# A decode layer on one core: the first weight load in eight pieces, a wait ahead of x, and eight unused matmuls before the last waits

## The chip, the core and the metric

The kernel runs on one NeuronCore of a Trainium2 chip. Its engines are PE (matmul; PEld is its weight load), DVE, ACT and POOL (elementwise work), and SP, which here only issues DMA transfers. Sixteen DMA engines move data between HBM and the on-chip memory. The metric is the device time of one execution in microseconds (us), the median over runs; lower is better.

## What is computed

One token goes through a pre-norm layer with grouped-query attention over a cache of 65536 positions, and a gated feed-forward block:

```
x: (1, 1, 1024)   Hq, Hkv, Sk, Dh = 32, 4, 65536, 128   F = 3584   all bf16
q = layernorm(x) @ wq                        # wq 1024 x 4096
scores = q . k_cache * Dh**-0.5              # 8 query heads share one cache head
o = softmax(scores) . v_cache                # k_cache, v_cache 4 x 65536 x 128
h = x + o @ wo                               # wo 4096 x 1024
n = layernorm(h)
out = h + (gelu(n @ w_gate) * (n @ w_up)) @ w_down   # 1024 x 3584 twice, 3584 x 1024
```

The two caches are 67.1 MB each, and everything is read once: 173 MB in all.

## The kernel before

All large data go through one buffer, `ring`, of four slots of 4 MB. The slots take, in order, the two halves of `wq` (slots 0 and 1), then K tiles (slots 2 and 3, two of 4 MB a step) and V tiles (slots 0 and 1, one of 8 MB a step) for eight steps (four cache heads, two halves of the positions each), then `wo` (slots 2 and 3), `w_gate` (0 and 1), `w_up` (2 and 3) and `w_down` (0 and 1). All of these transfers stand on SP's queue in that order, and each is issued as soon as the last reader of its slot has let go.

Work is written as a list of operations. `Flow.op` (line 31) notes which operations an operation depends on by the keys it reads (`r`) and writes (`w`), `Flow.dma` (line 69) does the same for a transfer, and `Flow.issue` (line 76) walks the list once and gives each engine its instructions and semaphore waits in the order of the list. Nearly all instructions therefore carry line 95 in the profile. Only the loop over the eight attention steps on PE is written out by hand (`pe_loop`, lines 411 to 449), and so is the last product.

**The start.** Line 200 issues the load of `x` (2 KB, 32 rows) on ACT's queue; it waits for nothing. Lines 202 to 205 issue the two halves of `wq` on SP's queue, each one transfer of 128 rows (one a partition) of 32 KB, with the semaphore `r_sem[t]`; a transfer adds 16 to its semaphore when it has landed. Lines 221 and 222 issue the first two K tiles behind them. `ones_f` (a 128 x 128 block of ones for sums across partitions) is set on DVE at line 226; it is DVE's first operation. `x` is then spread over the partitions (line 289), normalised (`layernorm_cols`, line 268) into `xz`, and multiplied with the halves of `wq` (lines 315 to 319), eight groups of four matmuls of 512 columns for each half.

**The end.** `w_down` comes in four transfers (lines 580 to 586), called wa, wb0, wb1 and wb2 here: 4 MB, 2 MB, 768 KB and 256 KB, each with a semaphore of its own. After the list is issued (line 588) a second block (lines 596 to 600) makes PE wait for one of these transfers after the other and multiply its rows: `down` (line 590) does eight matmuls of 128 columns for each row a partition holds, so 128 matmuls for wa, and 64, 24 and 8 for the others. They need `actz`, the gated activations, which DVE finishes behind the `w_up` product (line 574). Lines 602 to 604 copy the result out of the accumulators and store it.

`bank[5]` is one of PE's eight accumulators; its last reader is `o_copy` (line 376) of the last attention step. `qs` (line 164) holds the spread-out queries, which nothing reads after the attention loop.

Of the kernel before, what the change touches and what calls it, by code (L numbers as in the profile page):

```python
# [16 lines left out]
class Flow:  # L17
# [13 lines left out]
    def op(self, e, call, r=(), w=(), after=(), wait=(), inc=None, dma=False, rows=None, **kw):  # L31
        i = len(self.ops)
        deps = {}

        def need(j, hard):
            o = self.ops[j]
            if o["e"] == e and not dma and not o["dma"] and (e == "pe" or not hard):
                return
            deps[j] = True

        for k in r:
            if k in self.writer:
                need(self.writer[k], True)
        for k in tuple(w) + tuple(after):
            if k in self.writer:
                need(self.writer[k], True)
            for j in self.readers.get(k, ()):
                need(j, False)
        if e == "pool":
            if self.rows[0] != rows and self.rows[1] is not None and not self.ops[self.rows[1]]["inc"]:  # L50
                deps[self.rows[1]] = True
            self.rows = rows, i
        last = {}
        for j in deps:
            o = self.ops[j]
            k = j if o["dma"] else o["e"]
            last[k] = max(last.get(k, j), j)
        deps = last.values()
        for k in r:
            self.readers.setdefault(k, []).append(i)  # L60
        for k in w:
            self.writer[k] = i
            self.readers[k] = []
        self.ops.append(dict(e=e, call=call, kw=kw, deps=sorted(deps), wait=wait, inc=inc, dma=dma))
# [44 lines left out]
def kernel(  # L109
# [13 lines left out]
    nc = tc.nc  # L123
    P = 128
# [6 lines left out]
    DC = D // P  # L131
# [14 lines left out]
    NB = 512  # L146
# [12 lines left out]
    def sb(name, shape, dtype=F32):  # L159
        return const.tile(shape, dtype, name=name)  # L160
# [3 lines left out]
    qs = sb("qs", [P, 4, NS, P + 1], BF16)  # L164
    sc = sb("sc", [P, CPH, NN, rep, NS])
    pt = sb("pt", [P, CPH, NN, rep, NS], BF16)
    bank = [psum.tile([P, NB], F32, name="bank%d" % i) for i in range(8)]
# [15 lines left out]
    def slot(i, n=1):  # L183
        return ring[:, i * CW:(i + n) * CW]

    f = Flow(nc, tc)
    op = f.op
# [4 lines left out]
    r_sem = [tc.alloc_semaphore("r_landed_%d" % i) for i in range(3)]  # L192


    wq_v = A_wq.rearrange("(p t c) n -> t p c n", t=DS, c=C4)
    assert C4 * HD == CW and DS * C4 == DC
    XU = 32
    XV = P // XU
    x_in = sb("x_in", [XU, XV, DC], BF16)
    f.dma("act", x_in[:], A_x[0, 0].rearrange("(u v j) -> u v j", u=XU, j=DC), w=["x_in"], sem=tc.alloc_semaphore("x_landed"))  # L200
    wq_tiles = []
    for t in range(DS):
        wv = slot(t).rearrange("p (c n) -> p c n", c=C4)
        f.dma("sp", wv, wq_v[t], w=["R%d" % t], sem=r_sem[t])
        wq_tiles.append(wv)
    k_v = [A_k_cache[0, g].rearrange("(p n) d -> p n d", p=P) for g in range(Hkv)]
    v_v = [A_v_cache[0, g].rearrange("(p n) d -> p n d", p=P) for g in range(Hkv)]
# [14 lines left out]
        k_load(0, p)  # L222


    ones_f = sb("ones_f", [P, P])
    op("dve", "memset", w=["ones_f"], ap=ones_f[:], constant=1.0)
    neg_half = sb("neg_half", [P, 1])
    op("dve", "memset", w=["neg_half"], ap=neg_half[:], constant=-0.5)
    ident_bf = sb("ident_bf", [P, P], BF16)
# [93 lines left out]
    for q in range(4):  # L323
        op("pe", "matmul", r=["q_bf"] + ["esel"], w=["B5"], out=qsel_ps[:, :, q, :], lhsT=esel[:, q, :], rhs=q_bf[:],
           start=True, stop=True)
# [162 lines left out]
    for dq in range(OQ):  # L488
        op("pe", "matmul", r=["o_sb", "osel"], w=["B4"], out=o2_ps, lhsT=osel[:, dq, :], rhs=o_sb[:, dq * Hq:(dq + 1) * Hq],
           start=(dq == 0), stop=(dq == OQ - 1))  # L490
# [8 lines left out]
    FA = CW // D  # L499
    FB = FC - FA  # L500
    at_ps = bank[6][:]
    wv = slot(2, 2).rearrange("p (c n) -> p c n", c=Hq)
    f.dma("sp", wv, A_wo.rearrange("(p c) n -> p c n", p=P), w=["R2", "R3"], wait=done, sem=r_sem[2])
    for c in range(Hq):
        for s in range(DS):
            q = 2 * (c % 2) + s
            op("pe", "matmul", r=["o2z", "R2", "R3"], w=["B6"], out=at_ps[32 * q:32 * q + 32, :], lhsT=o2z[:, c, :],
               rhs=wv[:, c, :].rearrange("k (p s c) -> k s p c", s=DS, c=C4)[:, s], start=(c < 2), stop=(c >= Hq - 2), tile_position=(0, 32 * q))
# [55 lines left out]
    for j in range(DC):  # L564
        op("pe", "matmul", r=["hb", "sel16"], w=["B2"], out=d_ps[:, j:OB:DC], lhsT=hb[:, j, :], rhs=sel16[:],
           start=False, stop=False, skip_group_check=True)
# [15 lines left out]
    for i, z in enumerate((FB - FZ, FZ - 1, 1)):  # L582
        part = wb[:, e0:e0 + z, :]
        s = (r_sem[1], k_sem[0], k_sem[1])[i]
# [5 lines left out]
    def down(a_row, w_row):  # L590
        for j in (0, 4, 1, 5, 2, 6, 3, 7):
            q, m = divmod(orow[j], 32)
            nc.tensor.matmul((d_ps, d_odd)[q // 2][32 * q:32 * q + 32, :], lhsT=a_row[:, AZ - m:AZ - m + 32], rhs=w_row[:, j * OB:(j + 1) * OB],  # L593
                             start=False, stop=False, skip_group_check=True, tile_position=(0, 32 * q))

    with tc.tile_critical(no_gpsimd_drain=True):
        for w_rows, a0, n, at, sem in parts:
            nc.tensor.wait_ge(sem, at)
            for e in range(n):
                down(actz[:, a0 + e, :], w_rows[:, e, :])  # L600
# [34 lines left out]
```

## Time and profile before

| | us |
|---|---|
| median of 3 runs (lowest, highest) | 410.23 (409.99, 410.27) |
| the profiled execution's own time | 410.4 |
| its span, first to last instruction | 408.3 |
| PE busy, 1639 matmuls | 233.4 |
| DVE busy | 202.6 |
| ACT busy | 39.5 |
| POOL busy | 19.2 |
| one 128 x 4096 transpose of K on DVE (32 of them) | 4.418 |
| `x`: median from issue to landing | 2.1 |
| a half of `wq`: median from issue to landing | 16.8 |
| a 4 MB K tile: median from issue to landing | 24.6 |

The span is shorter than the time of the execution by 2.1 us, which lie around the instructions. Busy times of different engines overlap. The clock column of the profile, PEclk, is the share of TensorE's full clock that was granted; its mean over the span is 0.776. A landing is the moment at which the last of the sixteen DMA engines has reported its share.

### The profile page before, as it was taken

The page shows a single profiled execution, that of the slowest core. Times are in us where ns is not written, and L with a number is a line of the kernel's source. Part 1 is how long each engine was busy: PE and PEld are TensorE (multiplying, and loading weights), DVE is VectorE, ACT ScalarE, POOL GpSimd, SP SyncE. Part 2 cuts the span into 40 slices and gives each one's busy share as a digit, 9 for nine tenths or more (in the row PEclk, how much of TensorE's full clock was granted, in tenths as well). Part 3 has the DMA queues.
Part 4 walks back from the last instruction along what each step waited for, and adds up shares of the span by engine and source line. Part 5 has one row for each costly group of instructions (what it writes and reads, how often), then busy time and mean ns, then how long its engine had stood idle before and what let it go on. Part 6 is the DMA issues. An engine that isn't in the chain of part 4 may idle for free. (4 is left out here: it accounts for less than half of the span.)

```text
span 408.3 us, 3895 instructions
## 1 busy us (share of the span) xinstructions
PE 233.4 (57%) x1639; PEld 105.8 (26%) x1639; DVE 202.6 (50%) x174; ACT 39.5 (10%) x141; POOL 19.2 (5%) x39
## 2 busy tenths in 40 slices
PE   1331864684667368736973585558557737355356
PEld 1110322231322133213321232223223213132325
DVE  4016780886089327924881697087608941021110
ACT  1000003001300300030003000400030030000000
POOL 6010000001000000010000001000000000011000
PEclk9955895699669876976797899679866997565565
DMA  8999999999999999999999999999999999899994
GB/s 337 433 424 445 424 453 411 459 411 431 440 459 417 411 441 478 417 404 421 498 417 392 430 443 433 417 459 417 427 433 469 411 417 494 386 440 440 400 422 198
DMA packets 4815, 173.12 MB, mean 424 GB/s; under 512 B 580, under 2 KB 584, under 8 KB 840
## 3 DMA queue, kind: packets, MB, share of 16 engines
q1 hardware_dynamic: 4760, 173.02, 98.4%
q8 instruction: 5, 0.08, 0.1%
q14 instruction: 2, 0.02, 0.0%
q10 hardware_dynamic: 48, 0.00, 0.0%
HBM read 173.02 MB, written 0.00 MB: 424 GB/s over the span
## 5 line engine op out<-in xcount | busy, mean ns | idle before, releaser
L95 DVE STREAM_TRANSPOSE ktb<-ring 128x4096 f32<-128x4096 f32 x32 | 141.1, 4418 | 82.8 <-DMA ring<-in_A_k_cache_dram 82.8
L427 PE MATMUL bank<-ktb,qs 128*128 128x512 bf16 x512 | 132.9, 419 | 60.3 <-PEq L413 60.3
L427 PEld LDWEIGHTS bank<-ktb,qs 128*128 128x128 bf16 x512 | 51.6, 104 | 138.4 <-issue 93.0
L439 PE MATMUL bank<-ring,pt 128*32 128x512 bf16 x512 | 46.6, 543 | 36.5 <-PEq L413 36.5
L95 ACT ACTIVATE pt<-sc,nb 128x256 bf16<-128x256 f32 x64 | 31.5, 493 | 254.8 <-DVE nb L95 254.8
L439 PEld LDWEIGHTS bank<-ring,pt 128*32 128x32 bf16 x512 | 19.4, 131 | 60.4 <-issue 57.5
L95 DVE STREAM_TRANSPOSE sc<-bank 128x512 f32<-128x512 f32 x32 | 22.3, 695 | 24.9 <-PE bank L427 24.9
L95 PE MATMUL bank<-ring,xz 128*32 128x512 bf16 (+1 forms) x192 | 18.3, 565 | 24.0 <-DMA ring<-in_A_wq_dram 13.3
L95 DVE STREAM_TRANSPOSE ktb<-bank 128x512 f32<-128x512 f32 (+1 forms) x6 | 4.0, 672 | 37.3 <-PE bank L95 37.0
L95 DVE TENSOR_REDUCE mx<-sc 128x8 f32<-128x1536 f32 (+1 forms) x16 | 19.5, 1220 | 0.5
L95 POOL COPY qs<-qsel 32x128 bf16<-32x128 bf16 x16 | 7.8, 490 | 237.4 <-PE bank L427 216.4
L95 PEld LDWEIGHTS bank<-ring,xz 128*32 128x32 bf16 x192 | 7.0, 137 | 33.8 <-DMA ring<-in_A_wq_dram 14.2
L95 ACT ACTIVATION_READ_ACCUMULATOR pt<-sc,nb 128x1 f32 x64 | 11.9, 186 | 0.0
L448 PE MATMUL bank<-sel,acc_sb 128*128 128x8 f32 x64 | 8.2, 255 | 6.2 <-PEq L413 6.2
L431 PE MATMUL bank<-ident_f,mx 128*8 128x128 f32 x8 | 2.2, 269 | 14.6 <-PEq L413 14.6
L448 PEld LDWEIGHTS bank<-sel,acc_sb 128*128 128x128 f32 x64 | 7.7, 191 | 10.0 <-issue 10.0
L95 PE MATMUL bank<-ring,ktb 128*32 128x512 bf16 x64 | 6.0, 548 | 6.8 <-DMA ring<-in_A_wo_dram 6.8
L593 PE MATMUL bank<-ring,ktb 128*32 128x128 bf16 x224 | 6.6, 311 | 5.4 <-DMA ring<-in_B_w_down_dram 5.4
L95 ACT COPY acc_sb<-bank 128x512 f32<-128x512 f32 x8 | 4.7, 586 | 49.2 <-PE bank L439 49.2
L95 DVE TENSOR_TENSOR h_col<-bank,x_col 128x8 f32<-128x8 f32 x1 | 0.2, 166 | 15.2 <-PE bank L95 15.2
L95 PE MATMUL bank<-sel,ktb 128*128 128x16 f32 (+1 forms) x24 | 5.6, 374 | 3.5 <-DVE bank L95 2.7
L593 PEld LDWEIGHTS bank<-ring,ktb 128*32 128x32 bf16 x224 | 5.8, 144 | 6.4 <-DMA ring<-in_B_w_down_dram 6.1
(83 smaller groups left out, 55.2 us busy)
## 6 DMA issues: line engine op xcount, KB each, us to landing
ring<-in_A_k_cache_dram SPq DMA_DIRECT2D x16, 4096.0 KB, 24.6
ring<-in_A_wq_dram SPq DMA_DIRECT2D x2, 4096.0 KB, 16.8
ring<-in_B_w_gate_dram SPq DMA_DIRECT2D x1, 7168.0 KB, 27.8
ring<-in_B_w_up_dram SPq DMA_DIRECT2D x1, 7168.0 KB, 27.7
ring<-in_B_w_down_dram SPq DMA_DIRECT2D x1, 4096.0 KB, 20.9
ring<-in_B_w_down_dram SPq DMA_DIRECT2D x1, 2048.0 KB, 25.4
ring<-in_B_w_down_dram SPq DMA_DIRECT2D x1, 768.0 KB, 26.1
ring<-in_B_w_down_dram SPq DMA_DIRECT2D x1, 256.0 KB, 26.2
```

Source lines behind the costliest of these rows:

```text
L95: ins = getattr(self.eng[e], o["call"])(**o["kw"])
L427: m = nc.tensor.matmul(bank[c][:], lhsT=qs[:, jt].rearrange("p s c -> p (s c)")[:, s * P:(s + 1) * P], rhs=mv[:, :, J, :, u], start=(s == ...
L431: nc.tensor.transpose(out=mxT_ps, in_=mx1[:], identity=ident_f[:]).then_inc(s_step, 1)
L439: m = nc.tensor.matmul(acc[32 * q:32 * q + 32, :], lhsT=pt[:, c, n, :, :].rearrange("p h s -> p (h s)"), rhs=v_sb[:, c, :, n, :], start=(c ...
L448: m = nc.tensor.matmul(o_ps, lhsT=acc_sb[:, u * Dh:(u + 1) * Dh], rhs=sel[:, u:SQ:NS], start=(u == 0), stop=(u == NS - 1))
L593: nc.tensor.matmul((d_ps, d_odd)[q // 2][32 * q:32 * q + 32, :], lhsT=a_row[:, AZ - m:AZ - m + 32], rhs=w_row[:, j * OB:(j + 1) * OB], sta ...
```

## The change

Three edits are made together.

1. The first half of `wq` is issued as eight transfers of 16 rows, where transfer j takes partitions j, j+8, j+16 and so on. All eight add to `r_sem[0]`; only the last counts as the writer of the slot, so readers wait for the sum of all eight. The second half stays one transfer.
2. The set of `ones_f` moves to the front of the list, and the load of `x` names it as a key it reads, so ACT waits for DVE's memset before it issues the load.
3. In the last block PE does four matmuls of 128 x 128 by 512 columns ahead of the wait for wa, and four more ahead of the wait for wb0 (`a0` is 0 for wa and `FA` for wb0). They read `qs` and write `bank[5]`, and nothing reads the result.

```diff
     x_in = sb("x_in", [XU, XV, DC], BF16)
-    f.dma("act", x_in[:], A_x[0, 0].rearrange("(u v j) -> u v j", u=XU, j=DC), w=["x_in"], sem=tc.alloc_semaphore("x_landed"))
+    ones_f = sb("ones_f", [P, P])
+    op("dve", "memset", w=["ones_f"], ap=ones_f[:], constant=1.0)
+    f.dma("act", x_in[:], A_x[0, 0].rearrange("(u v j) -> u v j", u=XU, j=DC), w=["x_in"], r=["ones_f"], sem=tc.alloc_semaphore("x_landed"))
     wq_tiles = []
     for t in range(DS):
         wv = slot(t).rearrange("p (c n) -> p c n", c=C4)
-        f.dma("sp", wv, wq_v[t], w=["R%d" % t], sem=r_sem[t])
+        step = 8 if t == 0 else 1
+        for j in range(step):
+            f.dma("sp", wv[j::step], wq_v[t][j::step], w=["R%d" % t] if j == step - 1 else [], sem=r_sem[t])
         wq_tiles.append(wv)
...
-    ones_f = sb("ones_f", [P, P])
-    op("dve", "memset", w=["ones_f"], ap=ones_f[:], constant=1.0)
     neg_half = sb("neg_half", [P, 1])
...
+    def stay_busy(n):
+        for i in range(n):
+            nc.tensor.matmul(bank[5][:], lhsT=qs[:, 0, 0, 0:P], rhs=qs[:, 1 + i % 3].rearrange("p s c -> p (s c)")[:, 0:NB], start=True, stop=True)
+
     with tc.tile_critical(no_gpsimd_drain=True):
         for w_rows, a0, n, at, sem in parts:
+            stay_busy({0: 4, FA: 4}.get(a0, 0))
             nc.tensor.wait_ge(sem, at)
             for e in range(n):
                 down(actz[:, a0 + e, :], w_rows[:, e, :])
```

## The prediction, made before the changed kernel was run

> **What bounds the kernel.** I read the page first, its DMA rows above all.
>
> ```profile
> span 408.3 us, 3895 instructions
> ...
> DMA  8999999999999999999999999999999999899994
> ...
> q1 hardware_dynamic: 4760, 173.02, 98.4%
> ```
>
> The sixteen DMA engines are busy in every slice but the first and the last, and SP's queue (q1) fills 98.4% of them. The page's issues show a 4 MB K tile landing 24.6 us after its issue, while 4 MB alone take 9.7 us (below), so some 15 us of transfers are always queued ahead. What shifts the stream as a whole shifts the end; what PE or DVE does in the middle does not, until it is 15 us late. So two places decide: how soon the stream starts, and what remains to be done when it ends. For the start I read the timeline.
>
> ```profile
> 0.97 0.40 ACTq L95 DMA_DIRECT2D x_in<-in_A_x_dram  x1
> 1.01 0.86 SPq L95 DMA_DIRECT2D ring<-in_A_wq_dram  x2
> ...
> 1.93 1.00 SPq L95 DMA_DIRECT2D ring<-in_A_k_cache_dram  x2
> ...
> 3.25 0.18 PEld L95 LDWEIGHTS bank<-x_in,xsel 32*128 32x128 bf16 x4 [3.25 <-DMA x_in<-in_A_x_dram]
> ...
> 6.96 1.77 DVE L95 TENSOR_SCALAR xz<-ln_xc,ln_rstd 128x8 bf16<-128x8 f32 x1 [0.68 <-POOL ln_rstd L95]
> ...
> 13.25 3.60 PE L95 MATMUL bank<-ring,xz 128*32 128x512 bf16 x32 [7.16 <-DMA ring<-in_A_wq_dram]
> ...
> 22.95 3.60 PE L95 MATMUL bank<-ring,xz 128*32 128x512 bf16 x32 [6.10 <-DMA ring<-in_A_wq_dram]
> ```
>
> The halves of wq are there at 13.24 and 22.95, 9.71 us apart: that is what 4 MB take in the stream. The first half's issue began at 1.01, 12.23 us before it was there, so **12.23 - 9.71 = 2.52 us** went into getting started. No DMA byte of the weights moves before 2.0 (the stretch 1.5 to 2.0 shows 0 GB/s). For the end I read the timeline and the granted clock by stretches (the column before the last two).
>
> ```profile
> 396.00:396.33 0.33, 0.00 (x0) 0.00 (x0) 0.00 (x0) 0.00 (x0) 0.00 (x0) 1.00 0.81 348
> 396.33:397.00 0.67, 0.00 (x0) 0.00 (x0) 0.00 (x0) 0.00 (x0) 0.00 (x0) 0.50 0.92 391
> ```
>
> ```profile
> 387.98 5.62 PE L95 MATMUL bank<-ring,xz 128*32 128x512 bf16 x64 [5.04 <-DMA ring<-in_B_w_up_dram]
> ...
> 397.68 3.61 PE L593 MATMUL bank<-ring,ktb 128*32 128x128 bf16 x128 [4.08 <-DMA ring<-in_B_w_down_dram]
> ...
> 402.57 3.08 PE L593 MATMUL bank<-ring,ktb 128*32 128x128 bf16 x96 [1.29 <-DMA ring<-in_B_w_down_dram]
> ```
>
> PE waits for wa until 397.68 and for wb0 until 402.57. From there the 96 matmuls of wb0, wb1 and wb2 run without another wait for a transfer, 3.08 us, at half the clock, which had fallen at 396.33, 2.7 us after the w_up product. wb1 and wb2 are 1 MB, 2.43 us at the stream's 432 GB/s (4 MB in 9.71 us), so they are there at about 405.0, and PE ends at 405.65: **PE's last eight matmuls are only just behind the transfers**.
>
> **The change, part by part.**
>
> *The first transfer.* Nothing in the trace is a 16-row transfer at the head of an empty queue. The nearest row is x: 32 rows, same moment, 2.1 us from issue to landing, nearly all of it startup. The farther one is the store at the end (4 rows): issued at 406.19, waited for until about 407.4, so 1.2 us. If startup goes from 2.52 to 2.1 the stream gains 0.42; by the store's row it would gain 1.3. The other bound: eight transfers have seven boundaries more. wb2's matmuls (8 of the 96, at 0.027 us from one start to the next, and 0.31 for the last to end) began at 405.65 - 0.31 - 7 x 0.027 = 405.15, so wb2 was there by then; 1 MB should have been there at 402.53 + 2.43 = 404.96, so the two boundaries within it cost at most 0.19, or 0.09 each; seven cost 0 to 0.65. I take a gain of **0.42**, by x, the row nearest in place and size, and nothing for the boundaries, since the stream shows no dip where it passes from the first half of wq to the second (524 GB/s in 12 to 13, 492 in 13 to 14). Ends: +0.65 and -1.3.
>
> *SP's queue.* Seven more issues at about 0.4 us (0.86 for two) put the second half of wq and both K tiles 3 us later on the queue. Cover: the first half, 9.7 us of transfers. Queued behind them is only the V load at 26.68, which waits for PE anyway. Cost 0; if a piece were issued later than its predecessor ended (1.2 us, an eighth of 9.71), the stream would pause, but 0.4 is a third of that.
>
> *x waits.* DVE's memset runs 1.11 to 1.28, so x is issued near 1.4 instead of 0.97, and its packets meet the stream of wq, each engine's first piece of which lasts about an eighth of 9.71, 1.2 us. Late by 0.4 to 2.5 us; behind it on ACT's queue stands only the table load (1.41), used first in the attention. xz is ready at 8.73 and the first half of wq at 13.24: 4.5 us of cover. Without it, PE would still have its 6.10 us of waiting for the second half. Cost 0. The memset's move changes nothing: it was DVE's first operation already.
>
> *The unused matmuls.* A group of sixteen 128 x 128 by 512 matmuls of the attention took 3.63 us at the full clock (50.63 on), 0.22 each; at half clock a group of four tiles of 512 columns takes 3.60 / 8 less the tail, 0.43. So four cost 0.87 at full and 1.71 at half clock. The first four come between 393.60 and 397.68, whether PE may start at once or only behind DVE's last product (395.28): 0. The second four follow wa's 128, whose last group starts at 400.96 and streams 0.11: at half clock they end at 401.07 + 1.71 = 402.78, **0.2 after** wb0's landing; at full clock long before it.
>
> What they do to the clock: in three stages of the trace the clock rose 4.7 (371.11 to 375.84), 4.9 (387.98 to 392.92) and 5.8 us (38.93 to 44.76) after PE had begun work without a gap. Before, wa's matmuls last 3.6 us and then PE idles 1.3. With the second four PE has no gap from 397.68 on, so the clock is full by 402.4 to 403.5 even if the first four achieve nothing. Half of the 96 matmuls or more then run at twice the rate, PE catches up with the transfers, and the end is wb2's landing (about 405.05) plus the last eight at full clock, half of 0.50: 405.3 instead of 405.65. I take **-0.3**. Ends: -0.35 and +0.2 (clock stays at half, the four in the way).
>
> [...] Here it fell after 2.6 and 2.7 us of idleness (376.63 to 379.26, 393.60 to 396.33). [...]
>
> **Sum.** -0.42 - 0.3 = -0.72. The profiled execution: 410.4 (span 408.3 and 2.1 around it), which would be 409.7; it lies 0.17 above the median, so against the median 410.23 the forecast is **409.5**. 0.2% is 0.82 us, about what a measurement of this kernel can tell from no change.
>
> **Rivals.**
>
> A, the forecast, 409.1 to 409.9: chance 0.45.
>
> B, the start gains what the store's row allows: first packets leave 0.7 to 1.3 us earlier. For it: the store's first bytes move 0.7 us after its issue (406.9), those of wq 1.0 after theirs, and the first 1 us of the stream, 2.0 to 3.0, starts packets for 526 GB/s while 3.0 to 4.0 starts 131, so the first packets are slow ones. Against: x with a quarter of the rows needed the same 1.0. 410.23 - 1.0 - 0.3 = 408.9. Chance 0.25.
>
> C, the clock stays at half and the second four stand in the way: 410.23 - 0.42 + 0.2 = 410.0. Against it: the rises above. Chance 0.12.
>
> D, the first edit does nothing, because all first packets wait for the same thing, whatever their number (x and wq moved first bytes at the same time): 410.23 - 0.3 = 409.9. Chance 0.1.
>
> E, the other side: each boundary within the first half stalls every DMA engine, because the next piece does not start until the one before is reported. Place: 2 to 14 us; price seven times the stall. It outweighs the gains from 0.72 / 7 = 0.1 us each, just past the bound from w_down; at 0.25 each the time is 410.23 + 1.75 - 0.72 = 411.3. Against: the pieces of w_down show no such stall. Chance 0.08.
> [...]
>
> **How the numbers follow.** Faster by over 0.82 needs B, or A with a start gain over 0.5: 0.25 + 0.11 = 0.36. Slower is E and a little of C with boundary costs: 0.09. The rest, 0.55, is within. The range 408.7 to 410.5 leaves out E and the far half of B, under 0.2; A's own is 409.1 to 409.9.
>
> **What would show it.** The first half of wq there at about 12.8, the second again 9.7 later; x later but xz ready before wq; PE's wait for wb0 ending near 402.1; the clock at 1.00 by then or within 1.5 us; last matmul 0.3 after wb2. The forecast is wrong if wq is there at 13.2 or later, or under 12.3, or if the clock is 0.50 to the end.

## The result, and the profile after

The changed kernel takes **420.54 us** (420.35 to 421.04, 5 runs) against 410.07 (409.85 to 410.27, 5 runs) before: the ratio is 1.0254, with a 95% interval of 1.0239 to 1.0268. It is 10.5 us slower, where 0.7 us faster was forecast. The profiled execution took 420.6 us, its span is 418.5.

The page after, lines of the slices (each about 10.5 us), of the queue and of the span:

```profile
span 418.5 us, 3916 instructions
...
DMA  9989999999999999999998999999999999899995
GB/s 194 207 354 448 468 429 404 432 467 401 417 435 451 413 436 432 429 442 429 432 482 376 438 482 420 398 432 467 413 420 470 407 420 476 388 440 433 427 418 218
...
q1 hardware_dynamic: 4872, 173.02, 98.5%
```

The same row before:

```profile
GB/s 337 433 424 445 424 453 411 459 411 431 440 459 417 411 441 478 417 404 421 498 417 392 430 443 433 417 459 417 427 433 469 411 417 494 386 440 440 400 422 198
```

The DMA row says "busy" in the first two slices as everywhere, and SP's queue fills 98.5%. The row below gives the loss away: 194 and 207 GB/s in those two slices (before: 337 and 433), 354 in the third, and from the fourth on some 430, as before. Busy did not mean the usual pace here: over 4 to 12 us the busy share is 0.97 at 197 GB/s, before 1.02 at 442. The timeline after, at the places that the prediction spoke of:

```profile
1.03 5.64 SPq L95 DMA_DIRECT2D ring<-in_A_wq_dram  x9
...
1.31 0.38 ACTq L95 DMA_DIRECT2D x_in<-in_A_x_dram  x1
...
6.72 0.18 PEld L95 LDWEIGHTS bank<-x_in,xsel 32*128 32x128 bf16 x4 [6.72 <-DMA x_in<-in_A_x_dram]
...
10.40 1.77 DVE L95 TENSOR_SCALAR xz<-ln_xc,ln_rstd 128x8 bf16<-128x8 f32 x1 [0.68 <-POOL ln_rstd L95]
...
23.94 3.56 PE L95 MATMUL bank<-ring,xz 128*32 128x512 bf16 x32 [14.42 <-DMA ring<-in_A_wq_dram]
...
33.56 3.61 PE L95 MATMUL bank<-ring,xz 128*32 128x512 bf16 x32 [6.06 <-DMA ring<-in_A_wq_dram]
```

The first half of `wq` is there at 23.94 instead of 13.24 us: 10.7 later, the whole loss. The second half, one transfer as before, comes 9.6 us behind it, at the usual pace (before 9.71). From the first half's arrival to the issue of the store it is 416.39 - 23.94 = 392.45 us, before 406.19 - 13.24 = 392.95: the rest of the kernel is 0.5 us shorter. So the time went in one place, the eight transfers, and they ran slowly rather than late: their first bytes move in the stretch from 2.4 to 2.5 us, 0.4 us later than those of the weights before.

### The profile page after: what moved, and what is told of

Same layout as the page of the kernel before. It is cut to its first block, busy times and chain, and to the rows that moved or that the text cites. A ratio compares the mean times of both kernels' runs of the same rounds, so it can differ in the third digit from the quotient of the medians.

```text
span 418.5 us, 3916 instructions
## 1 busy us (share of the span) xinstructions
PE 229.4 (55%) x1645; PEld 103.1 (25%) x1647; DVE 202.5 (48%) x174; ACT 39.5 (9%) x141; POOL 19.2 (5%) x39
## 3 DMA queue, kind: packets, MB, share of 16 engines
q1 hardware_dynamic: 4872, 173.02, 98.5%
## 5 line engine op out<-in xcount | busy, mean ns | idle before, releaser
L429 PE MATMUL bank<-ktb,qs 128*128 128x512 bf16 x512 | 130.7, 414 | 62.8 <-PEq L415 62.8
L441 PE MATMUL bank<-ring,pt 128*32 128x512 bf16 x512 | 45.6, 533 | 36.5 <-PEq L415 36.5
L95 POOL MEMSET ktb<- 128x1024 bf16 (+2 forms) x3 | 3.5, 1165 | 75.7 <-PE bank L429 75.7
L435 PE MATMUL bank<-diag,ones_f 8*128 8x8 f32 x16 | 3.5, 286 | 5.7 <-PEq L415 5.7
```

Of the source, the lines that this page charges most:

```text
L95: ins = getattr(self.eng[e], o["call"])(**o["kw"])
L429: m = nc.tensor.matmul(bank[c][:], lhsT=qs[:, jt].rearrange("p s c -> p (s c)")[:, s * P:(s + 1) * P], rhs=mv[:, :, J, :, u], start=(s == ...
L435: nc.tensor.matmul(bc_ps, lhsT=ones_f[0:rep, :], rhs=diag[:], start=True, stop=True).then_inc(s_step, 1)
L441: m = nc.tensor.matmul(acc[32 * q:32 * q + 32, :], lhsT=pt[:, c, n, :, :].rearrange("p h s -> p (h s)"), rhs=v_sb[:, c, :, n, :], start=(c ...
```

## The experiments

Three theories stood for the slow eight transfers. Z: a price for each transfer, or a low rate of small ones (rival E of the prediction). S: sixteen reads at once from places that collide. P: what counts is which partitions are written at a time.

P says nothing of why: what in the memory could make one set of partitions slower than another, no run shows. All runs are of the kernel before with one edit, unless said otherwise. A ratio is to the kernel before, with its 95% interval.

### One edit at a time

**The first edit alone:** the loop of the change, `x` and the last product as before.

> The kernel before with the first edit alone: eight transfers of 16 rows, every eighth partition. The changed kernel's first half of wq was there at 23.94 instead of 13.24 us, 10.7 later, and the whole was 10.5 slower. If that edit carries the loss: 420.3 to 421.2, first half there at 23.5 to 24.2. If the wait of x or the unused matmuls carry part of it: below 419.

420.66 us, ratio 1.0259 (1.0242 to 1.0276); first half there at 24.02. The first edit carries the whole loss.

**The other two alone:** one transfer for the first half, the wait of `x` and the unused matmuls as in the change.

> The changed kernel with the first half of wq as one transfer again: the wait of x and the eight matmuls alone. If the first edit carries the whole loss: 409.5 to 410.1 (the store was issued 0.5 us earlier, counted from the arrival of the first half, than before). If the rest carries part: over 411.

409.88 us, ratio 0.9994 (0.9984 to 1.0003): no change that can be told.

### What is slow about the eight transfers

**Eight transfers over all partitions.**

```diff
-        f.dma("sp", wv, wq_v[t], w=["R%d" % t], sem=r_sem[t])
+        step = 8 if t == 0 else 1
+        for j in range(step):
+            cut = slice(j * CW // step, (j + 1) * CW // step)
+            f.dma("sp", wv.rearrange("p c n -> p (c n)")[:, cut], wq_v[t].rearrange("p c n -> p (c n)")[:, cut], w=["R%d" % t] if j == step - 1 else [], sem=r_sem[t])
```

> The first half as eight transfers of the same 0.5 MB, but each over all 128 partitions (4 KB of each row). Theory Z (a price for each transfer or a low rate of small ones): again about 420.5, first half there at about 24. [...]

410.97 us, ratio 1.0017 (1.0007 to 1.0026), first half there at 14.16: 0.9 us later than as one transfer, not 10.7. S, with neighbouring rows read at once, and P, with all 128 partitions written by every piece, both leave it near the time of one transfer. Neither eight transfers nor their 0.5 MB are the cause; Z falls. What is left of it is 0.9 us, here with pieces of 4 KB where the others have 32 KB; whether the seven boundaries or the smaller pieces cost it was not parted.

**Eight transfers of sixteen neighbours.**

```diff
-            f.dma("sp", wv[j::step], wq_v[t][j::step], ...)
+            f.dma("sp", wv[j * (P // step):(j + 1) * (P // step)], wq_v[t][j * (P // step):(j + 1) * (P // step)], ...)
```

(against the loop of the change)

> The first half as eight transfers of 16 neighbouring partitions each. [...] Theory Z: as with every eighth partition, 420.5. Theory S: the reads are 64 KB apart, no loss: about 410.

436.3 us, ratio 1.0646 (1.0626 to 1.0666), first half there at 39.20. Still slower, where Z has 420.5 and S about 410. P leaves room for it; that sixteen neighbours would be the slower set, no run had shown. S could be saved by saying that reads 64 KB apart are the bad ones; the next two runs part them.

**Write and read exchanged.** One run writes every eighth partition and reads sixteen neighbouring rows (`wv[j::step]` from the rows `16 j` to `16 j + 15`), the other the reverse.

> Eight transfers of 16 rows that write every eighth partition, as in the change, but read 16 neighbouring rows of wq (64 KB apart, 1 MB in all), so rows of wq stand in other partitions than x expects. [...] Theory S, which after the run with neighbours must say that reads 64 KB apart are the slow ones: as that run, 435 to 437, first half there near 39.

420.46 us, ratio 1.0252 (1.0218 to 1.0286), first half there at 23.71. P, with the same partitions written as in the change, has it as the change, which had 420.54 us and 23.94.

> The reverse: 16 neighbouring partitions are written, every eighth row (512 KB apart) is read, so rows of wq stand in other partitions than x expects. Theory P: as the run with neighbours, 435 to 437, first half there near 39. Theory S: as the change, 420 to 421, first half there near 24.

435.94 us, ratio 1.063 (1.0593 to 1.0667), first half there at 39.62. The time goes with the partitions that are written, not with the rows that are read. The stretches 4 to 12 and 12 to 20 us (the last three columns are the granted clock, the DMA engines' busy share and GB/s) show it, first of the run that writes every eighth partition from neighbouring rows, then of the reverse:

```profile
4.00:12.00 8.00, 1.15 (x4) 0.97 (x4) 2.67 (x6) 0.00 (x0) 4.15 (x8) 1.00 0.98 201
12.00:20.00 8.00, 0.00 (x0) 0.00 (x0) 0.00 (x0) 0.00 (x0) 0.00 (x0) 1.00 1.08 225
```

```profile
4.00:12.00 8.00, 1.29 (x8) 1.03 (x6) 3.17 (x8) 0.00 (x0) 4.16 (x8) 1.00 1.14 131
12.00:20.00 8.00, 0.00 (x0) 0.00 (x0) 0.00 (x0) 0.00 (x0) 0.00 (x0) 1.00 1.00 115
```

The busy share, a mean over all sixteen DMA engines, is 0.98 to 1.14 in both, which gives no sign of an engine left out; the rate is 201 to 225 GB/s where every eighth partition is written and 115 to 131 where sixteen neighbours are. The same stretches of the kernel before have 442 and 451:

```profile
4.00:12.00 8.00, 1.15 (x4) 0.98 (x4) 2.67 (x6) 0.00 (x0) 4.15 (x8) 1.00 1.02 442
12.00:20.00 8.00, 3.60 (x32) 1.05 (x32) 0.00 (x0) 0.00 (x0) 0.00 (x0) 1.00 1.04 451
```

**Two halves of 64 partitions.** `step = 2`, neighbouring partitions.

> Two transfers of 64 neighbouring partitions each. [...] If only small pieces or far-apart partitions are slow: 410 to 411.

420.68 us, ratio 1.0258 (1.0225 to 1.029), first half there at 23.78. Two transfers of 2 MB are as slow as the eight of 0.5 MB over every eighth partition (420.66 us, 24.02): neither small pieces nor partitions far apart are needed for the loss.

**Every fourth partition.** `step = 4` in the loop of the change: four transfers of 32 rows.

> Four transfers of 32 rows, every fourth partition. [...]

410.39 us, ratio 1.0003 (0.9991 to 1.0014), first half there at 13.47. The stretches of this run:

```profile
4.00:12.00 8.00, 1.15 (x4) 0.98 (x4) 2.67 (x6) 0.00 (x0) 4.16 (x8) 1.00 1.07 459
12.00:20.00 8.00, 3.60 (x32) 1.08 (x32) 0.00 (x0) 0.00 (x0) 0.00 (x0) 1.00 0.92 397
```

With partitions 4 apart, 32 to a piece, the rate is that of one transfer: 459 GB/s in 4 to 12 us, where the kernel before has 442. Whether pieces four apart would keep it was open until this run; why they do and pieces eight apart do not, and how the rows are dealt to the DMA engines, were not seen.

### What the other two edits do by themselves

**The wait of x alone.**

> The kernel before with the wait of x alone. With both other edits away x landed only at 9.5 us, yet nothing waited for it at the end. If that wait is free: 409.9 to 410.3. If getting x out of the way starts the stream sooner (second packets of the DMA engines 0.1 earlier in the run with edits two and three): 409.8 to 410.0. If the late x costs: over 410.5.

409.98 us, ratio 0.9998 (0.9989 to 1.0007). `x` was there at 9.51 instead of 3.25, and nothing came of it. With both the wait and the unused matmuls, where `x` was there at 9.47, the timeline shows who paid:

```profile
13.15 1.77 DVE L95 TENSOR_SCALAR xz<-ln_xc,ln_rstd 128x8 bf16<-128x8 f32 x1 [0.68 <-POOL ln_rstd L95]
...
15.07 3.60 PE L95 MATMUL bank<-ring,xz 128*32 128x512 bf16 x32 [2.79 <-DVE xz L95]
...
22.81 3.60 PE L95 MATMUL bank<-ring,xz 128*32 128x512 bf16 x32 [4.14 <-DMA ring<-in_A_wq_dram]
```

PE now waits for `xz`, not for the first half of `wq`, and starts on it at 15.07, 1.8 us late; its wait for the second half shrinks from 6.10 to 4.14 us and takes it all.

**The unused matmuls alone.**

> The kernel before with the eight unused matmuls alone. If they keep the clock full for the last matmuls and that is worth what the trace of both edits showed (store issued 3.35 instead of 3.62 after wb0's arrival): 409.7 to 410.0. If the instruction wait within wb0 eats it: 410.0 to 410.2. If they stand in the way: over 410.3.

410.01 us, ratio 1.0001 (0.9992 to 1.001): nothing that can be told. The end of its timeline:

```profile
397.74 3.59 PE L593 MATMUL bank<-ring,ktb 128*32 128x128 bf16 x128 [1.43 <-DMA ring<-in_B_w_down_dram]
...
402.66 0.62 PE L593 MATMUL bank<-ring,ktb 128*32 128x128 bf16 x30 [0.36 <-DMA ring<-in_B_w_down_dram]
403.94 1.48 PE L593 MATMUL bank<-ring,ktb 128*32 128x128 bf16 x66 [0.65 <-issue]
...
405.12 0.12 PEld L593 LDWEIGHTS bank<-ring,ktb 128*32 128x32 bf16 x8 [0.28 <-DMA ring<-in_B_w_down_dram]
...
405.98 0.35 SPq L609 DMA_DIRECT2D out_dram<-h  x1
```

The first 30 matmuls of wb0 take 0.62 us instead of some 1.1 (30 at 0.027 and 0.31 for the last to end), as in the changed kernel, where the granted clock is 1.00 meanwhile (412.97 to 413.60). Then PE idles 0.65 us for nothing that the profile shows ("issue"); before, the 96 stand in one group without such a gap. That idling does not decide the end: the weight loads of the last eight matmuls wait for wb2 until 405.12, and the last matmul ends 0.30 us behind that, at 405.42 (before 405.65). The store is issued 3.32 us after PE took up wb0, 3.62 before: 0.3 us at most.

**The change with every fourth partition.**

```diff
-        step = 8 if t == 0 else 1
+        step = 4 if t == 0 else 1
```

(against the changed kernel)

> The changed kernel with four transfers of 32 rows, every fourth partition, instead of eight of 16, every eighth; nothing else differs. Theory P: the whole loss is gone with this one number: 409.6 to 410.3, first half of wq there at 13.0 to 13.6, a gain of 10.3 to 10.9. If the first edit cost anything else (issues on SP's queue, boundaries): 410.5 to 415.

410.2 us, ratio 1.0 (0.9991 to 1.0009), first half there at 13.56. One number, 8 or 4, decides over the 10 us. No version beat the kernel before by more than can be measured.

## Why the prediction was wrong, point by point

**What bounds the kernel: right.** The stream of transfers does; a delay of 10.7 us at its head reached the end as 10.5.

**The first transfer: the step that failed.** Its cost was bounded by the boundaries between transfers, 0 to 0.65 us for seven, and what a piece itself moves at was not asked: the prediction charged every byte the rate of 4 MB over all 128 partitions. None of its rows showed another set of partitions at that rate: the pieces of `w_down`, used as proof, go over all 128 partitions each. In its place the runs show that eight pieces of every eighth partition move 4 MB in about 20 us instead of 9.7, because of the partitions that are written: with writes and reads exchanged, the time went with the writes. What makes some sets of partitions slower, the runs do not show.

**The expected gain at the start: not there.** The 0.42 us taken from the row of `x` did not come. The stream does not start sooner with 16 rows in the first transfer: packets at the stream's pace start at 2.0 us before and at 2.4 in the changed kernel. The fastest run with the first half in pieces, four of every fourth partition, has it there at 13.47, later than the single transfer's 13.24. Rival D was right that fewer rows do not shorten the start; why it came later was not tried.

**Rival E: right in sign and place, wrong in mechanism.** It had 411.3 us and a chance of 0.08. That the DMA engines stand still at the boundaries is not what the trace shows: in the changed kernel their busy share is 0.97 in 4 to 12 us and 1.10 in 12 to 20, while the rate is 197 and 229 GB/s. Eight pieces over all 128 partitions cost 0.9 us (14.16 against 13.24), and four of every fourth partition 0.2 (13.47); the 0.2 cannot be told in the whole time.

**SP's queue: the size was off, the cover held.** Nine issues took 5.64 us, 0.63 each, not 0.4; the K tiles were issued at 6.71 instead of 1.93, and the stream had work until 23.94.

**The wait of x: the size was off, the cover held.** "Late by 0.4 to 2.5 us" was 3.5 in the changed kernel and 6.2 to 6.3 where the first half is one transfer: the one piece per engine, 1.2 us, that `x` was to wait behind was the author's estimate, and what it did wait behind was not shown. With one transfer it used up the 4.5 us of cover, and then part of the 6.10 us behind it; in the changed kernel `xz` was ready at 12.17, far ahead of the first half.

**The unused matmuls: the end as forecast, the gain too small to tell, and sized on one trace.** The clock was full for the last matmuls of the changed kernel, as forecast:

```profile
414.00:415.00 1.00, 0.77 (x42) 0.60 (x45) 0.00 (x0) 0.00 (x0) 0.00 (x0) 1.00 0.21 82
415.00:416.00 1.00, 0.72 (x32) 0.37 (x30) 0.00 (x0) 0.00 (x0) 0.00 (x0) 1.00 0.06 16
```

(The clock is the third column from the right.) From the start on wb0 to the store the profiles show 3.42 us instead of 3.62, so 0.2 where 0.3 was taken, and the runs with these matmuls alone cannot be told from the kernel before. The last matmuls did end just behind wb2, as forecast: at 415.82, with wb2 there at 415.53. Rival C did not happen. But the price was taken from one profile, in which the clock was 0.50 from wb0's arrival to the last matmul. The run with every fourth partition, which has none of these matmuls, ends much like it: its last 96 took 3.03 us (3.08 before), and the store came 3.57 us after the start on wb0. The three ends with these matmuls (the changed kernel, edits two and three, the unused matmuls alone) all have the first 30 in 0.62 us, and the store comes after 3.42, 3.35 and 3.32 us. Whether the clock is at half at the end of every execution without them was not shown.

## What to carry to other kernels

Here a transfer's rate went with the partitions it wrote together: in 4 to 12 us, pieces of every fourth partition moved 459 GB/s, one transfer over all 128 moved 442, pieces of every eighth 197 to 205, of 64 neighbours 197 and of 16 neighbours 131. So before a transfer is cut by rows, the set of partitions in a piece is the thing to try. When a transfer is cut, take the price of a piece from a row with the same set of partitions, and where no such row exists, let the range reach to the rates found here, a half (197 to 233 GB/s) and about a quarter (98 to 131) of the whole transfer's 442 to 451. And read GB/s beside the busy share: the share was 0.97 while the rate was 197 GB/s, and 1.02 at 442.

## What the runs showed of the hardware that was not expected

- Pieces of sixteen neighbouring partitions moved 98 to 131 GB/s, and pieces of every eighth partition or of 64 neighbours 197 to 233, in stretches of 8 us before the first half was there (4 to 12 and 12 to 20 us, for sixteen neighbours also 24 to 32), with a busy share of 0.85 to 1.14. The first half's arrival agrees: 23.7 to 24.0 us for every eighth partition and for 64 neighbours, 39.2 and 39.6 for sixteen neighbours, less than twice as late.
- A 2 KB load issued 0.3 us after the first 4 MB transfer landed 6.2 us later than one issued 0.04 us ahead of it (9.47 against 3.25).
- A full clock did not shorten the last 96 matmuls by half: in the changed kernel, with the clock at 1.00, they took 2.85 us from the first start to the last end, against 3.08 at 0.50 before. PE idled 0.43 and 0.21 us within them, the first for a reason that was not tried, and the last eight then waited for wb2. With the unused matmuls alone they took 2.76 us, with 0.65 idle.
